# A sigmoid-attention and gated feed-forward kernel: its steps and loads in one table laid out anew

## The chip, the cores and the metric

The kernel runs on one core of a Trainium2 chip. The metric is the device time of one execution in microseconds (us). Before the change it is 368.44 us, the median of three runs (368.12 to 368.74). One further execution was recorded by the hardware profiler; every duration below is from it, and its span, from the first instruction to the last, is 367.6 us.

## The reference, cut to what matters

Sigmoid attention over 8 batches, 12 heads, 448 positions and 64 dimensions; its output, taken as 3584 rows of 768, goes through a two-layer network with a gate:

```python
scores = scale * np.matmul(q, k.transpose(0, 1, 3, 2)) - np.log(S)
attn = 1.0 / (1.0 + np.exp(-scores))
x = np.matmul(attn, v)                        # heads side by side: 3584 x 768
h = x @ w_in                                  # 768 -> 2048
g = h * (1.0 / (1.0 + np.exp(-beta * h)))
out = g @ w_out                               # 2048 -> 768
```

All inputs and the output are fp32. The kernel loads them as fp16 (the DMA casts) and sums in fp32.

## The kernel before, in words

**Units of work.** A batch has 12 heads. Four heads are a quad `g` (three quads a batch, `QPB`), two heads are a slot. The kernel is one long list of steps, in an order written out by hand, that every engine follows for its own part: TensorE (PE), VectorE (DVE), ScalarE (ACT), GpSimd (POOL), and the DMA queues of GpSimd (loads with a cast) and SyncE (SP, the stores). No scheduler moves anything: each engine runs its instructions in the order in which the steps are called, and waits on semaphores for the others. A step is a letter with numbers, and `RUN` (L615) gives the function of each letter:

- `V g.jt` (`visit`, L243): the scores of a quad for one block of 128 keys, 8 or 16 matmuls of 32 rows, into score tiles in PSUM, and on ACT the sigmoid of each (`weigh`, L230). `half_visit` (L259) does the same for half of the queries (224); the first batch uses it.
- `A g` (`attend`, L282): the attention weights times the values, 64 columns wide, for all four key blocks, and the casts to `xT` on DVE (L303). The last block has 64 keys; its matmuls stand at the end, and for odd slots they read a copy of the values' last rows that `double_v_last` (`E`, L148) makes on DVE.
- `D b.dc` and `first_half` (`dense1`, L308): the first layer of batches 0 and 1, six matmuls, a sigmoid on ACT and a product on DVE. `O` (`dense2`, L341) is the second layer of the first two row tiles.
- `I` and `U` (`wino1` L432, `wino2` L530): the two layers of all other rows by seven products for a 2x2 block in place of eight. They need sums of tokens (`X`), of hidden values (`H`) and of weights (`S`, `T`), which DVE makes in fp16 from SBUF (all through `add`, L375), and gates: `G` and `B` (L495, L505) put the product of gate and value on POOL.
- `R g.r` (`transpose`, L194) turns queries (r = 0) or keys (r = 1) on DVE, `Q`, `K` and `load_...` issue loads on POOL's queue.

**PSUM.** `bank` (L89) hands out single banks, the one longest unused first; two score tiles (three in the opening) hold two banks each, so a visit waits until ACT has read the tiles of the visit before. `share_psum` (L76) lays the banks out anew after the opening.

**Tile form of the dense products.** `follow` (L641) looks ahead from each step to the next `V` or `A`. If that is an `A`, `dense` (L171) issues every product as two of 64 columns, the form in which `attend` runs, else as one of 128.

**SBUF rings.** Output tiles `osb` come from a ring of four (`outp`, L63): two for each `I` block or `U` pair, so a tile waits for the store of the one two blocks earlier. Stores go out on SP (L605), 32 rows each except in the last batch. Raw queries and keys have a ring of three, values of two.

**The opening** (L747 to L834) is code, not part of the list: ten matmuls on zeros (`idle_units`), the first quad's casts and turns, all loads up to the first layer's weights, then six half visits with 3, 4, 4, 4, 2 and 2 idle matmuls behind them, the three attends of the first query half with half visits between them, the beta turns, eight loads (L810 to L817: quads 3 and 4, values of batch 1, `w_out` in four parts with quad 5 between), and then the first layer of the first half with the second half's visits and attends between. `follow(STEPS)` runs the rest.

Of the kernel before, what the change touches and what calls it, by code (L numbers as in the profile page):

```python
# [13 lines left out]
def kernel(  # L14
# [267 lines left out]
    def attend(g: int, c0: int, n: int, part=(0, 1)):  # L282
# [4 lines left out]
        avs = [bank("av_ps") for _ in slots]  # L287
        order = sorted(range(JF), key=lambda jt: list(at_tiles).index((slots[-1], jt, c0)))
        todo = [(s, av, jt) for jt in order for s, av in zip(slots, avs)]
        for s, av, jt in todo + [(s, av, JF) for s, av in zip(slots, avs)]:  # L290
            at = at_tiles.pop((s, jt, c0))
            base, nk = (last_base(s), KL) if jt == JF else (0, P)
            for hh in range(2):
                nc.tensor.matmul(  # L294
                    av[hh * D : (hh + 1) * D, 0:n],
                    vs[b][base : base + nk, 2 * (s % NPAIR) + hh, jt],
                    at[base : base + nk, hh, 0:n],
                    start=(jt == order[0]),
                    stop=(jt == JF),
                    tile_position=(base, hh * D),  # L300
                )
        for s, av in zip(slots, avs):
            nc.vector.tensor_copy(out=xTs[b][:, s % NPAIR, c0 : c0 + n], in_=av[:, 0:n])  # L303
# [304 lines left out]
    todo = list(range(NDC))  # L608

    def first_half(n: int):  # L610
        for _ in range(n):
            dense1(0, todo.pop(0), 0, QH)

    ALSO = {g: (g + 1,) if g > QPB and g + 1 < NQUAD else () for g in range(QPB, NQUAD)}
    RUN = {  # L615
        "V": lambda g, jt: visit(g, jt, ALSO[g] if jt == JF else ()),
# [24 lines left out]
    def follow(steps):  # L641
        last_visit = max(i for i, step in enumerate(steps) if step[0] == "V")
        nearer = [""] * len(steps)
        for i in reversed(range(len(steps) - 1)):
            nxt = steps[i + 1][0]
            nearer[i] = nxt if nxt in "VA" else nearer[i + 1]
        for i, (step, then) in enumerate(zip(steps, nearer)):
            tiled["cols"] = D if then == "A" else P
# [5 lines left out]
        R3.1 R3.0 D0.6 D0.12 R4.1 D0.14 D0.7 V3.1 R4.0 D0.13 D0.0 D0.8 V3.0 D0.3 D0.9 V3.3 D0.1  # L654
        D0.10 E1 D0.2 Q6 V3.2 D0.4 O0.0.0 D0.5 O0.0.1 O0.0.2 V4.1 O1.0.0 O0.0.3 A3 V4.0 O1.0.1 R5.1
        D0.11 D0.15 O0.0.4 R5.0 V4.2 O0.0.5 S1.1 O0.0.6 O1.0.2 O1.0.3 S1.0 O0.0.7 S2.0 O1.0.4 V4.3
        O1.0.5 A4 V5.1 O1.0.6 O0.1.0 O0.1.1 O1.1.0 S2.1 Q7 T3.1 O1.0.7 S4.0 T2.1 O0.1.2 V5.0 T3.0
        O0.1.3 O1.1.1 K2 O1.1.2 O1.1.3 O0.1.4 O0.1.5 V5.2 T2.0 O1.1.4 O0.1.6 O0.1.7 R6.1 O1.1.5 R6.0
        A5 O1.1.6 I1.3.1 V6.2 O1.1.7 S4.1 D1.8 R7.0 S3.1 D1.11 T1.1 Q8 V6.0 Q9 D1.3 R7.1 D1.2 X1.0
        V6.1 D1.10 D1.9 E2 K3 D1.1 X1.1 V6.3 T1.0 D1.0 A6 V7.1 I1.3.6 I1.3.2 X1.2 I1.3.5 V7.0 X1.3  # L660
        I1.3.7 I1.3.3 I1.2.1 I1.3.4 G1.3 I1.2.6 B1.3.0 V7.2 R8.1 I1.2.5 I1.2.7 R8.0 B1.3.1 I1.2.2
        I1.2.3 I1.2.4 V8.0 U2.1.0 H2.2 B1.2.1 B1.2.0 R9.1 U2.1.1 R9.0 A7 V8.1 H2.0 H2.1 T4.1 T4.0
        U2.7.0 U2.2.0 U2.2.1 Q10 V8.2 U2.5.0 U2.6.0 U2.6.1 X2.0 S3.0 H2.3 E3 V8.3 U2.5.1 A8 G1.2
        X2.1 V9.1 U2.7.1 U2.3.0 U2.3.1 H4.0 I2.0.1 R10.0 V9.2 H4.2 I2.0.6 U2.4.0 I2.0.5 U2.4.1
        I2.0.2 H4.1 I2.0.3 R10.1 X2.2 U4.1.0 V9.0 X2.3 U4.1.1 Q11 G2.0 U4.6.0 U4.6.1 Q12 A9 V10.0
        I2.0.7 H4.3 U4.5.0 U4.7.0 U4.5.1 V10.1 U4.7.1 I2.0.4 B2.0.1 U4.3.0 U4.4.0 U4.2.0 B2.0.0
        U4.2.1 R11.0 U4.3.1 U4.4.1 R11.1 I2.1.1 V10.2 Q13 Q14 I2.1.6 I2.1.5 I2.1.7 I2.1.2 K4 I2.1.3
        V10.3 I2.1.4 G2.1 B2.1.0 R12.1 I2.2.1 B2.1.1 A10 V11.0 I2.2.6 I2.2.5 R12.0 I2.2.7 I2.2.2
        I2.2.3 I2.3.1 Q15 G2.2 V11.1 I2.3.6 I2.2.4 B2.2.1 B2.2.0 I2.3.5 I2.3.2 R13.1 I2.3.7 I2.3.3
        V11.2 I2.3.4 B2.3.1 U6.1.0 B2.3.0 H6.2 U6.1.1 A11 H6.0 V12.2 U6.2.0 U6.7.0 H6.1 U6.2.1 G2.3  # L670
        V12.0 X3.0 U6.5.0 U6.6.0 U6.6.1 X3.1 U6.5.1 H6.3 I3.0.1 U6.7.1 I3.0.6 X3.2 V12.1 H8.0 E4
        R13.0 U6.3.0 U6.3.1 U6.4.0 U6.4.1 I3.0.5 R15.0 Q16 V12.3 H8.2 I3.0.2 A12 H8.1 V13.1 I3.0.3
        R14.0 U8.1.0 U8.1.1 U8.5.0 U8.6.0 G3.0 I3.0.7 U8.6.1 V13.0 X3.3 R15.1 H8.3 U8.2.0 R14.1
        U8.2.1 U8.5.1 U8.7.0 V13.2 U8.7.1 U8.3.0 I3.0.4 U8.4.0 R16.1 B3.0.0 B3.0.1 U8.3.1 V14.0
        U8.4.1 I3.1.1 A13 V14.1 I3.1.6 K5 I3.1.5 I3.1.7 I3.1.2 I3.1.3 I3.2.1 I3.1.4 Q18 I3.2.6 G3.1
        B3.1.0 B3.1.1 I3.2.2 I3.2.5 V14.2 I3.2.7 I3.2.3 Q17 I3.3.1 I3.2.4 G3.2 I3.3.6 I3.3.5 B3.2.0
        B3.2.1 I3.3.2 I3.3.7 I3.3.3 V14.3 I3.3.4 U10.1.0 B3.3.0 B3.3.1 H10.2 R16.0 U10.1.1 A14 V15.2
        U10.2.0 H10.0 U10.7.0 H10.1 G3.3 U10.2.1 U10.5.0 U10.6.0 U10.6.1 H10.3 U10.5.1 X4.0 V15.0
        U10.7.1 X4.1 U10.3.0 U10.3.1 I4.0.1 I4.0.6 I4.0.5 H12.0 U10.4.0 X4.2 U10.4.1 X4.3 I4.0.2
        I4.0.3 I4.0.7 V15.1 E5 K6 G4.0 Q19 H12.2 U12.1.0 H12.1 U12.1.1 A15 R17.0 V16.1 U12.2.0 R18.1  # L680
        I4.0.4 B4.0.0 U12.6.0 B4.0.1 U12.2.1 U12.5.0 V16.2 U12.6.1 U12.5.1 I4.1.1 H12.3 I4.1.6
        U12.7.0 U12.7.1 R17.1 I4.1.5 U12.3.0 U12.3.1 I4.1.2 V16.0 R18.0 I4.1.3 U12.4.0 I4.1.7
        U12.4.1 Q20 G4.1 V16.3 I4.1.4 A16 B4.1.0 B4.1.1 R19.0 V17.2 I4.2.1 I4.3.1 I4.2.6 I4.2.5
        V17.1 I4.2.2 Q21 I4.2.7 I4.2.3 G4.2 V17.0 I4.2.4 I4.3.6 B4.2.0 I4.3.5 I4.3.7 I4.3.2 B4.2.1
        R20.0 I4.3.3 G4.3 V18.2 I4.3.4 R19.1 A17 I5.0.1 B4.3.0 X5.0 B4.3.1 U14.1.0 V18.0 I5.0.2 X5.1
        I5.0.6 Q22 I5.0.5 U14.1.1 V18.1 X5.2 X5.3 H14.0 I5.0.3 U14.2.0 E6 H14.2 K7 I5.0.7 H14.1
        V18.3 G5.0 U14.2.1 A18 V19.2 I5.0.4 U14.6.0 U14.5.0 U14.7.0 B5.0.0 U14.6.1 U14.5.1 B5.0.1
        U14.7.1 I5.1.1 V19.0 H14.3 I5.1.6 I5.1.2 U14.3.0 R21.1 U14.3.1 R20.1 V19.1 U14.4.0 E7 I5.1.5
        I5.1.7 U14.4.1 I5.1.3 V20.0 R21.0 I5.1.4 G5.1 B5.1.0 I5.2.1 B5.1.1 A19 V20.2 I5.2.6 Q23
        I5.2.5 I5.2.2 I5.2.7 I5.2.3 I5.3.1 I5.2.4 G5.2 I5.3.6 B5.2.0 V20.3 I5.3.5 I5.3.7 B5.2.1  # L690
        I5.3.2 I5.3.3 I5.3.4 V20.1 X6.0 B5.3.1 H16.2 B5.3.0 U16.1.0 U16.1.1 A20 V21.2 U16.2.0 H16.0
        U16.7.0 U16.2.1 G5.3 V21.0 H16.1 U16.5.0 R23.1 U16.6.0 U16.6.1 H16.3 U16.5.1 U16.7.1 H18.2
        I6.0.1 X6.2 V21.1 U16.3.0 X6.1 U16.3.1 U16.4.0 U16.4.1 I6.0.6 R22.1 I6.0.2 R22.0 I6.0.5 A21
        V22.0 H18.0 X6.3 I6.0.3 H18.1 U18.1.0 U18.7.0 U18.1.1 V22.1 I6.0.7 U18.6.0 U18.6.1 V22.2
        I6.0.4 H18.3 U18.5.0 G6.0 U18.2.0 R23.0 U18.5.1 U18.2.1 B6.0.1 B6.0.0 U18.7.1 V22.3 U18.3.0
        U18.3.1 U18.4.0 U18.4.1 I6.1.1 I6.1.6 A22 V23.0 I6.1.5 I6.1.7 I6.1.2 I6.1.3 I6.2.1 G6.1
        I6.1.4 B6.1.0 I6.2.6 I6.2.5 B6.1.1 I6.2.2 V23.1 I6.2.7 I6.2.3 I6.3.1 I6.2.4 I6.3.6 G6.2
        B6.2.1 I6.3.5 B6.2.0 I6.3.7 I6.3.2 I6.3.3 V23.2 I6.3.4 B6.3.1 U20.1.0 H20.2 U20.1.1 A23
        U20.7.0 B6.3.0 U22.1.0 H20.0 U20.2.0 H20.1 X7.0 U20.2.1 U20.5.0 U20.6.0 G6.3 U20.6.1 I7.0.1
        U20.5.1 H20.3 X7.2 U22.1.1 U20.7.1 I7.0.2 X7.1 U20.3.0 U20.3.1 U22.2.0 U22.2.1 H22.0 U20.4.0  # L700
        X7.3 H22.2 H22.1 U20.4.1 U22.5.0 I7.0.6 I7.0.5 U22.7.0 I7.0.7 I7.0.3 U22.6.0 G7.0 I7.0.4
        I7.1.1 I7.1.6 I7.1.5 B7.0.0 B7.0.1 I7.1.2 I7.1.7 I7.2.1 I7.1.3 I7.2.6 G7.1 I7.1.4 I7.2.5
        I7.2.7 B7.1.0 B7.1.1 U22.6.1 I7.2.2 I7.2.3 U22.5.1 H22.3 I7.2.4 I7.3.1 I7.3.6 B7.2.0 I7.3.5
        G7.2 B7.2.1 I7.3.7 U22.7.1 I7.3.2 I7.3.3 U24.1.0 I7.3.4 U22.3.0 U22.3.1 U24.1.1 U22.4.0
        B7.3.0 U22.4.1 U24.2.0 B7.3.1 H24.0 U26.1.0 U24.2.1 H24.1 U24.5.0 G7.3 U24.6.0 H24.2 U24.6.1
        U24.5.1 H24.3 H26.0 U24.7.0 U24.7.1 U26.1.1 U24.3.0 U24.3.1 H26.1 U24.4.0 U26.2.1 U26.5.0
        U26.6.0 H26.2 U26.6.1 U26.5.1 H26.3 U26.7.0 U26.7.1 U24.4.1 U26.3.0 U26.3.1 U26.4.0 U26.4.1
        U26.2.0
# [7 lines left out]
    with tc.manual_schedule():  # L716
# [62 lines left out]
        for g in range(1, QPB):  # L779
            load_one(g, 0, 0, NH)  # L780
            load_one(g, 1)
        load_v(0)
        nc.sync.dma_start(out=beta_in[0:NDC], in_=moe_beta.rearrange("(c p) -> c p", p=P))
        for g in range(QPB - 1):
            load_one(g, 0, NH, NB)
        for c in range(WCH):
            if c == WCH // 2:
                load_one(QPB - 1, 0, NH, NB)
            load_w_in(c)
# [76 lines left out]
```

## Time and profile before

| what | value |
|---|---|
| median of three runs | 368.44 us (368.12 to 368.74) |
| span of the profiled execution | 367.6 us |
| instructions | 9130 |
| HBM read, written | 45.62 MB, 11.01 MB |
| DMA, mean over the span | 95 GB/s |
| PE's last group of matmuls | ends at 364.05 us |
| last store | issued at 364.5 us |

The page gives for each engine its busy time and the share of the span. A group's row gives its line, engine, operation and tiles, how many there are, how long they are busy, the mean of one, and the idle time of the engine before them with what ended it. Matmuls are pipelined, so the times of one overlap with the next; what a matmul costs PE is read from the distance of starts in the timeline. The median of the runs lies 0.84 us above the profiled span; both are needed to turn a sum made in the trace into a time.

### The profile page before, as it was taken

To read this page: it belongs to the slowest core of one execution; us is meant where nothing else is said; L and a number is where in the kernel's file an instruction comes from. 1 tells how busy PE (TensorE), PEld (TensorE's weight loads), DVE (VectorE), ACT (ScalarE), POOL (GpSimd) and SP (SyncE) were. 2 spreads that over 40 slices of the span, in tenths; PEclk is the share of its full clock that TensorE was granted. 3 is DMA by queue.
4 is the path that set the end of the run, shared out by engine and by line. 5 is a ranking of instruction groups with operands and counts; after the bars stand their busy time and mean duration, and the time that the engine had idled before them with its cause. 6 is when DMAs were issued, how large, how long until landed. Compare 5 with 4: busy or idle time off the path is not lost.

```text
span 367.6 us, 9130 instructions
## 1 busy us (share of the span) xinstructions
PE 361.6 (98%) x3677; PEld 237.7 (65%) x3677; DVE 272.2 (74%) x524; ACT 248.7 (68%) x410; POOL 154.3 (42%) x192
## 2 busy tenths in 40 slices
PE   8999999999999999999999999999999999999996
PEld 3478754457465685557757667666856688689763
DVE  4356569889995796876778678868879677778764
ACT  5987976789765797657865579977874859225410
POOL 7834523504413873117761445841630316216610
PEclk9999999999999999999999999999999999999999
DMA  8999999930363890517909363373303030030233
GB/s 163 182 197 201 197 206 199 237 40 2 50 139 52 165 147 2 81 57 122 143 9 153 52 137 51 50 79 88 52 1 88 2 87 2 0 87 0 61 67 134
DMA packets 42698, 34.76 MB, mean 95 GB/s; under 512 B 21904, under 2 KB 39200, under 8 KB 42656
## 3 DMA queue, kind: packets, MB, share of 16 engines
q0 software_dynamic: 36688, 22.47, 44.7%
q1 hardware_dynamic: 5968, 11.71, 11.5%
q8 instruction: 29, 0.48, 0.6%
q14 instruction: 13, 0.11, 0.1%
HBM read 45.62 MB, written 11.01 MB: 154 GB/s over the span
## 4 chain that ended last, share of the span: by engine, by line
PE 94%; DMA 3%; ACT 1%; DVE 1%; SPq 0%; issue 0%; ACTq 0%; DVEq 0%
PE m_ps L174 71%; PE sco L221 12%; PE av_ps L294 10%; DMA out_dram<-osb 2%; PE idle_ps L743 1%; ACT attnT L233 1%; DMA gt<-in_k_dram 1%; DVE osb L375 0%; SPq L605 0%; ACT osb L428 0%; DVE xT L303 0%; ACT osb L466 0%; DVE raw L760 0%; SPq L726 0%; DVE kT L763 0%
## 5 line engine op out<-in xcount | busy, mean ns | idle before, releaser
L233 ACT ACTIVATE attnT<-sco 128x896 f16<-128x896 f32 (+1 forms) x163 | 139.2, 908 | 38.5 <-PE sco L221 37.9
L375 DVE TENSOR_TENSOR osb<-m_ps,osb 128x448 f32<-128x448 f32 (+2 forms) x197 | 116.3, 596 | 51.7 <-PE m_ps L174 42.2
L174 PEld LDWEIGHTS <-w_in 128*128 128x128 f16 (+1 forms) x948 | 81.0, 100 | 19.4 <-issue 11.5
L174 PE MATMUL m_ps<-xT,w_in 128*128 128x224 f16 (+3 forms) x750 | 85.5, 266 | 0.8 <-ACT osb L466 0.5
L495 POOL TENSOR_TENSOR gt<-osb,sg 128x448 f16<-128x448 f32 x26 | 29.5, 1135 | 118.4 <-ACT sg L428 108.2
L505 POOL TENSOR_TENSOR gt<-osb,sg 128x448 f16<-128x448 f32 x52 | 58.3, 1137 | 34.9 <-ACT sg L428 33.2
L428 ACT ACTIVATE sg<-osb,beta_sb 128x224 f32<-128x224 f32 (+1 forms) x104 | 54.0, 575 | 10.0 <-DVE osb L375 9.8
L174 PEld LDWEIGHTS <-sum 128*128 128x128 f16 (+1 forms) x444 | 39.9, 99 | 27.4 <-issue 3.7
L174 PEld LDWEIGHTS <-gt 128*128 128x128 f16 (+1 forms) x474 | 36.9, 102 | 25.8 <-issue 7.7
L174 PE MATMUL m_ps<-w_out,gt 128*128 128x384 f16 (+2 forms) x350 | 52.6, 324 | 0.0
L221 PE MATMUL sco<-qT,kT 32*128 32x448 f16 (+3 forms) x864 | 51.4, 340 | 0.4 <-DVE kT L763 0.2
L174 PEld LDWEIGHTS <-w_S 128*128 128x128 f16 (+1 forms) x486 | 43.9, 99 | 7.0 <-issue 6.0
L174 PE MATMUL m_ps<-w_out,sum 128*128 128x384 f16 (+1 forms) x228 | 40.6, 327 | 0.0
L174 PE MATMUL m_ps<-w_T,sum 128*128 128x384 f16 (+1 forms) x216 | 40.3, 326 | 0.0
L303 DVE CAST xT<-av_ps 128x448 f16<-128x448 f32 (+1 forms) x54 | 28.4, 566 | 14.3 <-PE av_ps L294 14.1
L294 PE MATMUL av_ps<-attnT,v 128*64 128x448 f16 (+3 forms) x400 | 38.2, 343 | 0.0
L174 PE MATMUL m_ps<-xs,w_S 128*128 128x224 f16 (+1 forms) x330 | 36.2, 259 | 0.0
L294 PEld LDWEIGHTS <-v 128*64 128x64 f16 (+1 forms) x432 | 20.5, 108 | 18.1 <-issue 10.2
L428 ACT ACTIVATE osb<-m_ps,beta_sb 128x224 f32<-128x224 f32 x52 | 20.4, 449 | 15.3 <-PE m_ps L174 13.8
L221 PEld LDWEIGHTS <-kT 32*128 32x128 f16 (+1 forms) x864 | 13.4, 96 | 23.1 <-issue 20.9
L466 ACT COPY osb<-m_ps 128x448 f32<-128x448 f32 x26 | 13.8, 536 | 18.4 <-PE m_ps L174 15.4
L135 POOL DMA_DIRECT2D v<-in_v_dram x32 | 19.9, 633 | 13.3 <-DMA w_out<-in_moe_w_out_dram 6.5
(53 smaller groups left out, 300.5 us busy)
## 6 DMA issues: line engine op xcount, KB each, us to landing
out_dram<-osb SPq DMA_DIRECT2D x100, 96.0 KB, 2.6
raw<-in_k_dram POOLq DMA_DIRECT2D x23, 224.0 KB, 5.8
raw<-in_q_dram POOLq DMA_DIRECT2D x21, 224.0 KB, 4.5
v<-in_v_dram POOLq DMA_DIRECT2D x32, 144.0 KB, 7.4
w_in<-in_moe_w_in_dram POOLq DMA_DIRECT2D x8, 384.0 KB, 10.4
w_out<-in_moe_w_out_dram POOLq DMA_DIRECT2D x4, 768.0 KB, 13.1
v<-in_v_dram POOLq DMA_DIRECT2D x16, 48.0 KB, 6.2
out_dram<-osb SPq DMA_DIRECT2D x4, 192.0 KB, 2.6
```

The lines of the kernel that those rows point to most:

```text
L135: queue.dma_start(out=to[i * BLK : (i + 1) * BLK, h0:h1, 0:JF].rearrange("p h j d -> p h (j d)"), in_=rows[:, :, JF * i * D : JF * (i + 1) ...
L174: nc.tensor.matmul(to[c : c + step], hidden[:, c : c + step], weights, **({} if step == P else {"tile_position": (0, c)}), **flags,)
L221: nc.tensor.matmul(sco[base : base + nk, hh, u0 : u0 + n], kT[g][lo : lo + BLK, jt * P : jt * P + nk, e], qT[g][lo : lo + BLK, c0 : c0 + n ...
L233: nc.scalar.activation(out=at[:, :, 0:n], in_=sco[:, :, 0:n], func=AF.Sigmoid, bias=NEG_LOG_S, scale=MSCALE,)
L294: nc.tensor.matmul(av[hh * D : (hh + 1) * D, 0:n], vs[b][base : base + nk, 2 * (s % NPAIR) + hh, jt], at[base : base + nk, hh, 0:n], start ...
L303: nc.vector.tensor_copy(out=xTs[b][:, s % NPAIR, c0 : c0 + n], in_=av[:, 0:n])
L375: nc.vector.tensor_tensor(out=out, in0=in0, in1=in1, op=op)
L428: nc.scalar.activation(out=out, in_=in_, func=AF.Sigmoid, bias=0.0, scale=beta_sb[:, dc : dc + 1])
L466: nc.scalar.copy(out=oa[:, 0], in_=m)
L495: nc.gpsimd.tensor_tensor(out=gt[:, 2 * d : 2 * d + 2, off : off + QH], in0=ob[:, 0], in1=sg, op=ALU.mult)
L505: nc.gpsimd.tensor_tensor(out=gt[:, dc, off : off + S].rearrange("p (h n) -> p h n", h=2), in0=oa[:, :, j], in1=sg, op=ALU.mult,)
L743: nc.tensor.matmul(idle[:, 0:cols], still[:, 0:P], still[:, 0:cols], start=True, stop=True)
```

## The change

**One table.** The opening becomes a list of steps too (`OPENING`), and `follow(OPENING + STEPS)` runs both. `RUN` has new letters: `i` idle matmuls, `h` a half visit, `f` the first layer on the first query half, `r` half a turn, `l`, `k`, `v`, `w`, `o` loads, `b` the beta turns, `p` the PSUM layout. The number of idle matmuls stays at 29; the code ahead of the list stays as it is (the first quad's loads, casts and turns, and the first ten idle matmuls).

**Opening's values in two steps.** `attend` takes a `stage`: `y` does the first three key blocks and keeps the bank (`hold`), `z` the last block, the release and the casts.

```diff
-    def attend(g: int, c0: int, n: int, part=(0, 1)):
+    def attend(g: int, c0: int, n: int, part=(0, 1), stage=(0, 1)):
...
-        avs = [bank("av_ps") for _ in slots]
-        order = sorted(range(JF), key=lambda jt: list(at_tiles).index((slots[-1], jt, c0)))
-        todo = [(s, av, jt) for jt in order for s, av in zip(slots, avs)]
-        for s, av, jt in todo + [(s, av, JF) for s, av in zip(slots, avs)]:
+        if 0 in stage:
+            order = sorted(range(JF), key=lambda jt: list(at_tiles).index((slots[-1], jt, c0)))
+            for s in slots:
+                avs[s, c0] = bank("av_ps", hold=None if 1 in stage else (s, c0)), order[0]
+        todo = []
+        if 0 in stage:
+            todo += [(s, jt) for jt in order for s in slots]
+        if 1 in stage:
+            todo += [(s, JF) for s in slots]
...
+        if 1 not in stage:
+            return
+        for s in slots:
+            av, _ = avs.pop((s, c0))
+            if (s, c0) in held:
+                touch(held.pop((s, c0)))
```

**The look-ahead** sees the new letters, and takes the 64-column form ahead of `y` as well:

```diff
-            nearer[i] = nxt if nxt in "VA" else nearer[i + 1]
+            nearer[i] = nxt if nxt in "VAhyz" else nearer[i + 1]
...
-            tiled["cols"] = D if then == "A" else P
+            tiled["cols"] = D if then in ("A", "y") else P
```

**The order.** The opening's list:

```
i4 l1.0.0 k1 R1.1 l2.0.0 k2 v0 l0.0.1 l1.0.1 w0 w1 i3 i2 w2 w3 r1.0 l2.0.1 w4 w5 w6
h0.0.0 w7 R2.1 h0.0.1 i4 b0 h1.0.0 i4 h1.0.1 r2.0 h2.0.1 r0.1 i2 h2.0.0 y1.0 E0 z1.0
h0.1.1 y2.0 z2.0 r1.1 p0 Q3 Q4 o0.0 K1 o1.0 Q5 o0.1 o1.1 y0.0 z0.0 h0.1.0 f1 f0 f2
h1.1.0 f4 f5 f3 f6 h1.1.1 r2.1 f7 y0.1 z0.1 h2.1.0 f8 f9 f10 f11 h2.1.1 y1.1 z1.1
f12 y2.1 z2.1 f13
```

Nine of the 19 later idle matmuls (`i4`, `i3`, `i2`) now stand ahead of the first half visit `h0.0.0`. The rest of the table holds the same steps as before in another order; of the places that the prediction speaks of, these rows are before and after:

```
before  ... U8.3.0 I3.0.4 U8.4.0 ... U8.4.1 I3.1.1 A13 V14.1 I3.1.6 K5 ... Q18 ... Q17 I3.3.1 ...
after   ... I3.0.5 K5 A12 ... V13.2 Q18 ... U8.3.1 U8.4.0 B3.0.0 U8.4.1 A13 V14.1 I3.1.6 ...
before  ... V5.2 T2.0 O1.1.4 O0.1.6 O0.1.7 R6.1 O1.1.5 R6.0 A5 O1.1.6 I1.3.1 V6.2 ...
after   ... T3.0 T2.0 O1.1.1 O0.1.5 O1.1.2 R6.0 X1.0 O0.1.6 O1.1.3 V5.2 R6.1 T3.1 S2.1 O0.1.7
        O1.1.4 O1.1.5 T1.0 O1.1.6 A5 Q8 R9.1 V6.2 O1.1.7 K3 T1.1 D1.11 T2.1 S3.1 R7.1 ...
before  U26.7.0 U26.7.1 U24.4.1 U26.3.0 U26.3.1 U26.4.0 U26.4.1 U26.2.0
after   U26.7.0 U26.7.1 U26.3.0 U24.4.1 U26.4.0 U26.3.1 U26.4.1 U26.2.0
```

The fp16 sums (`X`, `H`, `S`, `T`) are placed at other steps than `G` and `B`, whose products run on POOL. What each step computes is the same.

## The prediction

> **What bounds the kernel now.** I read the page's first part, then the chain, then PE's waits.
>
> ```profile
> span 367.6 us, 9130 instructions
> ...
> PE 361.6 (98%) x3677; PEld 237.7 (65%) x3677; DVE 272.2 (74%) x524; ACT 248.7 (68%) x410; POOL 154.3 (42%) x192
> ...
> PE 94%; DMA 3%; ACT 1%; DVE 1%; SPq 0%; issue 0%; ACTq 0%; DVEq 0%
> ```
>
> PE is busy for 361.6 of 367.6 us and is 94% of the chain. What is left is 1.19 us ahead of the first matmul, some waits, and the last store. So the change can win only what PE loses inside its work, and can lose anywhere. PE's waits:
>
> ```profile
> PE idle_ps L743 <- DVE gt L736: 1.2, 1, 1.2
> PE m_ps L174 <- ACT osb L466: 0.5, 1, 0.5
> PE m_ps L174 <- ACT attnT L233: 0.2, 1, 0.2
> PE sco L221 <- DVE kT L763: 0.2, 1, 0.2
> PE sco L221 <- ACT attnT L233: 0.2, 1, 0.2
> ```
>
> After 19.4 us only the 0.5 us counts. The timeline between 177 and 182 us shows what is behind it:
>
> ```profile
> 177.51 0.79 ACT L428 ACTIVATE osb<-m_ps,beta_sb 128x224 f32<-128x224 f32 x2 [1.23 <-DMA out_dram<-osb]
> ...
> 178.53 1.31 PE L174 MATMUL m_ps<-xs,w_S 128*128 128x224 f16 x12
> ...
> 179.78 0.55 ACT L466 COPY osb<-m_ps 128x448 f32<-128x448 f32 x1
> ...
> 180.38 1.31 PE L174 MATMUL m_ps<-xT,w_in 128*128 128x224 f16 x12 [0.54 <-ACT osb L466]
> ...
> 181.77 0.73 PE L174 MATMUL m_ps<-xT,w_S 128*128 128x224 f16 x6
> ```
>
> ACT waits 1.23 us for a store to leave its output tile, so the copy at 179.78 is late and PE waits for it. Twelve such matmuls take 12 x 0.096 = 1.15 us; from 178.53 to 180.38 they took 1.85, from 180.38 to 181.77 1.39: 0.70 + 0.24 = 0.94 us lost. The stores are late because the loads of K5 (in the order, just behind U8's last stores) share the DMA engines: between 165 and 180 us stores take 2.9 to 6.0 us to land, against 1.8 where nothing loads.
>
> **Part 1, opening: +0.8 us.** PE's and ACT's timelines before:
>
> ```profile
> 1.19 4.03 PE L743 MATMUL idle_ps<-gt 128*128 128x512 f16 x10 [1.19 <-DVE gt L736]
> 5.42 0.58 PE L221 MATMUL sco<-qT,kT 32*128 32x224 f16 x16 [0.20 <-DVE kT L763]
> ...
> 19.37 2.46 PE L174 MATMUL m_ps<-xT,w_in 128*128 128x224 f16 x24 [0.21 <-ACT attnT L233]
> ```
> ```profile
> 6.04 6.28 ACT L233 ACTIVATE early<-sco 128x896 f16<-128x896 f32 x8 [0.87 <-PE sco L221]
> 12.46 3.06 ACT L233 ACTIVATE attnT<-sco 128x896 f16<-128x896 f32 x4
> 16.15 3.17 ACT L233 ACTIVATE attnT<-sco 128x896 f16<-128x896 f32 x4 [0.62 <-PE sco L221]
> ```
>
> From 6.04 to 15.5 us ACT never stops: it reads score tiles, and PE's half visits wait for it. The first product of the first layer (19.37) follows ACT's 16th sigmoid. After the change nine warm idle matmuls (0.216 us each from start to start, 1.04 for four with the change of form) come ahead of the first half visit: it starts at 4.95 + 0.11 + 9 x 0.216 + 0.10 = 7.10 instead of 5.42, and ACT's first sigmoid at 7.71 instead of 6.04, 1.67 late. I walk on with the distances of before. Sigmoids 1 to 8 keep their rhythm (the idle matmuls between them are the same 4 and 4): the eighth ends at 14.0. h2.0.1 needs the tile of the seventh (13.56): its sigmoids run from 14.36, those of h2.0.0 from 15.86 to 17.58. y1.0 and z1.0 stand on PE meanwhile (15.9 to 16.8; v landed at 14.05, its copy is done by 15.0). h0.1.1 starts at 16.85, its first sigmoid ends at 18.52. By the order's semaphores y0.0 waits for that one, for the new PSUM layout reuses the bank: 18.57. y0.0, z0.0 and h0.1.0 take 1.4 us, and f1 also waits for z0.0's two casts (0.7 us behind its last matmul): the first layer starts in effect at **20.2 instead of 19.37**. Behind it both kernels have the same first-layer work, and I find no step in which PE waits more than 0.1 us. Bounds: if ACT never waited for PE (14 sigmoids and their pitches of 0.81 and 0.43 from 7.71), y0.0 could start at 17.2, that is -0.5; if every hand-over costs another 0.1, +1.3.
>
> **Part 2, PE's own work: -0.4 us.** A matmul in the form of the one before costs 96 ns at 224 columns; going from one form to another costs about 0.1 us: from 22.27 to 24.10 us there are 18 matmuls and one change, 18 x 0.096 + 0.10 = 1.83.
>
> ```profile
> 22.27 1.90 PE L174 MATMUL m_ps<-xT,w_in 128*128 128x224 f16 x18
> 24.10 0.74 PE L221 MATMUL sco<-qT,kT 32*128 32x224 f16 x16
> ```
>
> Counting forms in the two orders from the first layer on: 189 changes before, 186 after, -0.3 us. The look-ahead also splits 104 more products in two of 64 columns; a pair takes 162 to 163 ns at 384 columns and 95 to 96 at 224, one whole 163 and 96: -0.1 at most, I take it. Bounds 0 to -0.5.
>
> **Part 3, the waits of the steady part: -1.05 us.** K5 now stands ahead of A12 and Q18 behind V13.2, some 13 and 7 us of PE's work ahead of U8's last stores; those then land in about 1.9 us and the 0.94 us go. Another 0.11 goes at 44.36, where PE's first `w_out` matmul waits for its load: o0.0 is now issued ahead of K1, which by the landings of before puts it at 40.4. For what is late next I compared every wait of PE with PE's work between it and its source. The shortest such distances are alike in both orders (1.25 us from a product to the use of its bank, 1.4 from an attend to its `xT`). The stores' tightest new place is U10.3.1 to U12.1.1, 5.5 us against 6.7 before, where the store landed 1.6 us early; 0.4 is left. I take no new wait there, with +0.5 as its bound.
>
> The fp16 sums away from POOL's products: 0. DVE waits little for POOL:
>
> ```profile
> DVE osb L375 <- PE m_ps L174: 42.2, 58, 2.2
> ...
> DVE sum L375 <- POOL gt L505: 1.2, 2, 0.7
> ```
>
> and it idles 42.2 us waiting for PE, so what a sum saves is covered. The Trainium skill, "SBUF — State Buffer", section "Who interferes with whom", says that a VectorE instruction with two SBUF inputs contends with a GpSimd instruction that reads SBUF, and that whichever issues first holds the pair while the other fully blocks. The trace agrees in that one sum alone overlaps a product by over 0.1 us (799 ns against 685); by the rule a meeting would cost up to a product's 1.14 us, and eight of them 9 us of VectorE, still less than its 42.2 us.
>
> **Part 4, a crowded queue of sums: +0.1.** Between 60 and 66 us the new order gives DVE, without a gap, T2.0, R6.0, X1.0, R6.1, T3.1, S2.1, an `osb` copy and T1.0, and then A5's two casts, which D1.11 needs 0.04 us after I expect them. I take 0.1; see the second rival.
>
> **Part 5, tail: +0.5 us.** The stores' last 864 KB flow without a gap at about 370 GB/s from 363.4 to 365.9. U24.4.1, whose 384 KB store opens that run, now comes one U part (four matmuls, 0.65 us) later, while PE's end stays. That delays the last landing by 0.5; bounds 0 and 0.65.
>
> **Sum.** +0.8 - 0.4 - 1.05 + 0.1 + 0.5 = -0.05: a span of 367.55, and with the 0.84 us between span and median **368.4 us**. From the bounds: -2.6 to +3.0 if all fell together.
>
> **Rivals.**
> - *The opening keeps ACT's pace* (faster). Then part 1 is -0.5 in place of +0.8: 367.1. For it: ACT, not PE, sets the opening's pace, and the new order puts visits next to each other. Against it: the walk above used the hand-overs that the trace shows.
> - *DVE's queue becomes the bound at 60 to 77 us* (slower). DVE is busy for 7.2 of the 8 us from 60 to 68 before, with four weight sums of 0.95 us there; now there are five, and three in place of two in the 8 us behind. By distances of starts the eight pieces of part 4 take 5.4 us, by their durations 6.3; the truth is between, and from 0.04 us on PE pays. At full durations PE loses 0.8 at D1.11 and 0.5 more before 77 us, +1.3: 369.7. Against it: starts are what a queue shows when it is full.
> - *The sums and products are not set apart in effect*, or were already: then no term changes, 368.4 too.
>
> **How the numbers follow.** A measurement can tell 0.2% (0.74 us) from no change. Forecast with its near cases, 367.7 to 369.2: 0.37. First rival, alone or with a smaller tail, 366.5 to 367.7: 0.33. Second rival or a store that comes late, over 369.2: 0.30. Those are the chances of same, faster, slower. The range leaves out 0.1 on either side: 366.8 to 370.0; the forecast's own is 367.7 to 369.2.
>
> **What would show it.** Part 1: the first `w_in` matmul at 20.2, ACT's first sigmoid at 7.7. Part 2: 0.1 us at each change. Part 3: no ACT wait for `out_dram<-osb` near 177, no PE wait for the copy behind it. Part 4: PE's wait on `xT` near 66. Part 5: 4.05 us from PE's end to the span's end, against 367.6 - 364.05 = 3.55. Wrong if PE shows a wait over 0.5 us that none of these names.

## The result, and the profile after

The changed kernel takes 372.64 us, the median of six executions (370.63 to 376.37). Against before the ratio is 1.0092, 95% interval 1.0065 to 1.012: slower by some 3.4 us, where 368.4 was predicted. The ratio leaves out disturbed executions (376.37 among them), so it is lower than that of the two medians. The profiled execution took 371.86 us at a span of 370.0. The lines of its page that answer to those shown of before:

```profile
span 370.0 us, 9330 instructions
...
PE 362.4 (98%) x3781; PEld 239.9 (65%) x3781; DVE 276.1 (75%) x524; ACT 247.9 (67%) x410; POOL 155.1 (42%) x192
...
PE 91%; POOL 2%; DVE 2%; DMA 1%; ACT 1%; issue 1%; SPq 0%; DVEq 0%; POOLq 0%
```

PE's share of the chain falls from 94 to 91%; POOL and DVE now have 2% each. PE's waits (in total, times, longest):

```profile
PE sco L221 <- ACT early L233: 1.5, 2, 0.9
...
PE m_ps L174 <- DVE sum L389: 0.6, 1, 0.6
PE m_ps L174 <- DVE xT L317: 0.6, 1, 0.6
PE sco L221 <- ACT attnT L233: 0.3, 1, 0.3
```

None of the first three stood before, the last was 0.2, and the 0.5 us for the copy at 180 us is gone. Put together by starts of matmuls in the two traces:

| us | before | after | difference |
|---|---|---|---|
| start to the first `w_in` matmul | 19.37 | 21.58 | +2.21 |
| from there to the start of the last matmul | 344.42 | 344.90 | +0.48 |
| from there to the end of the span | 3.78 | 3.56 | -0.22 |

The last row goes by the traces' spans to the hundredth, 367.57 and 370.04; with the rounded spans it is 3.81 and 3.52, and so the expectations below have it.

**The opening.** PE's timeline after:

```profile
7.46 0.67 PE L221 MATMUL sco<-qT,kT 32*128 32x224 f16 x18
9.04 0.69 PE L221 MATMUL sco<-qT,kT 32*128 32x224 f16 x14 [0.91 <-ACT early L233]
...
13.97 0.69 PE L221 MATMUL sco<-qT,kT 32*128 32x224 f16 x14 [0.64 <-ACT early L233]
...
16.43 1.66 PE L303 MATMUL av_ps<-early,v 128*64 128x224 f16 x16
...
21.58 2.09 PE L174 MATMUL m_ps<-xT,w_in 128*128 128x224 f16 x18
```

The first half visit starts at 7.46, not 7.10, and at 16.43 sixteen matmuls of the values take 1.66 us where such a group took 1.02 before. The trace's record of the granted clock says why: full clock from 5.62 us (4.89 before), half clock again from 15.858 to 19.271 us, 3.413 us, then full until PE is done. Before has no such stretch while PE works; its clock falls only at 366.70 us, behind the last matmul. The windows view, cut at multiples of 3.413 us from 5.62 (PE's busy time comes first, the granted clock behind the five engines):

```profile
9.03:12.45 3.42, 3.41 (x46) 1.42 (x45) 1.80 (x7) 3.27 (x5) 2.65 (x5) 1.00 1.69 183
12.45:15.85 3.40, 2.38 (x44) 0.96 (x40) 0.77 (x2) 3.04 (x5) 3.31 (x5) 1.00 1.40 193
15.86:19.27 3.41, 3.41 (x50) 1.81 (x44) 0.69 (x2) 2.05 (x4) 2.07 (x4) 0.50 1.40 173
```

In the stretch that holds the waits ahead of h2.0.1 and h2.0.0 PE was busy for 2.38 us; the next one ran at 0.50.

**The wait at 204.98 us.** The chain of waits between 198 and 206 us:

```profile
198.41 5.31 DMA out_dram<-osb
...
204.31 0.62 DVE xT L317
204.98 1.14 PE m_ps L174 x6
```

A store of U10, 5.3 us on its way, keeps its output tile; DVE's copy for U12.1.1 waits for it, and A15's casts wait behind the copy. On POOL's queue Q19's first load is issued just ahead of those stores, whose row on SyncE's queue follows, and before it was not:

```profile
196.09 0.58 POOL L115 DMA_DIRECT2D raw<-in_q_dram  x1
```
```profile
196.89 6.33 SPq L619 DMA_DIRECT2D out_dram<-osb  x8
```
```profile
202.10 1.14 POOL L495 TENSOR_TENSOR gt<-osb,sg 128x448 f16<-128x448 f32 x1 [7.74 <-DVE sum L375]
203.18 0.62 POOL L115 DMA_DIRECT2D raw<-in_q_dram  x1
```

The last two rows are before: Q19 stood behind the product of G4.0, which held POOL's queue for 7.74 us.

**The wait at 351.58 us.** DVE's and POOL's rows after:

```profile
349.20 1.60 DVE L389 TENSOR_TENSOR sum<-gt 128x1024 f16<-128x1024 f16 x1 [0.23 <-POOL gt L519]
```
```profile
349.12 1.14 POOL L509 TENSOR_TENSOR gt<-osb,sg 128x448 f16<-128x448 f32 x1
```

The sum H24.0 starts when POOL ends B7.3.1's product, and so does the next product, G7.3. The sum takes 1.60 us; its kind takes 0.69. Two steps later PE has waited 0.77 us (start to start, against its usual distance).

My theory: three causes, the nine early idle matmuls (over 2 us), Q19's new place (0.7 or more) and G7.3's new place (0.77), while the gain at 180 us belonged mostly to the one execution that I had profiled.

### The profile page after: what moved, and what is told of

Read it like the earlier page. It is cut to its first block, busy times and chain, and to the rows that moved or that the text cites. A ratio compares the mean times of both kernels' runs of the same rounds, so it can differ in the third digit from the quotient of the medians.

```text
span 370.0 us, 9330 instructions
## 1 busy us (share of the span) xinstructions
PE 362.4 (98%) x3781; PEld 239.9 (65%) x3781; DVE 276.1 (75%) x524; ACT 247.9 (67%) x410; POOL 155.1 (42%) x192
## 4 chain that ended last, share of the span: by engine, by line
PE 91%; POOL 2%; DVE 2%; DMA 1%; ACT 1%; issue 1%; SPq 0%; DVEq 0%; POOLq 0%
PE m_ps L174 68%; PE sco L221 12%; PE av_ps L303 10%; PE idle_ps L789 2%; POOL gt L519 2%; DMA out_dram<-osb 1%; ACT early L233 1%; DVE sum L389 1%; DVE osb L389 1%; SPq L619 0%; ACT attnT L233 0%; ACT sg L442 0%; DVE xT L317 0%; DVE gt L782 0%; DVE osb L584 0%
## 5 line engine op out<-in xcount | busy, mean ns | idle before, releaser
L174 PE MATMUL m_ps<-xT,w_in 128*128 128x224 f16 (+2 forms) x792 | 85.0, 265 | 0.0
L442 ACT ACTIVATE sg<-osb,beta_sb 128x224 f32<-128x224 f32 (+1 forms) x104 | 54.8, 578 | 5.8 <-DVE osb L389 5.7
L303 PEld LDWEIGHTS <-v 128*64 128x64 f16 (+1 forms) x432 | 21.4, 110 | 17.7 <-issue 9.6
L337 DVE TENSOR_TENSOR gt<-m_ps,sg 128x224 f16<-128x224 f32 (+1 forms) x40 | 16.1, 430 | 11.3 <-ACT sg L334 11.2
```

The costliest lines, as they stand in the source:

```text
L174: nc.tensor.matmul(to[c : c + step], hidden[:, c : c + step], weights, **({} if step == P else {"tile_position": (0, c)}), **flags,)
L303: nc.tensor.matmul(av[hh * D : (hh + 1) * D, 0:n], vs[b][base : base + nk, 2 * (s % NPAIR) + hh, jt], at[base : base + nk, hh, 0:n], start ...
L337: nc.vector.tensor_tensor(out=gt[:, dc, off : off + n], in0=m1[:, 0:n], in1=sg[:, 0:n], op=ALU.mult)
L442: nc.scalar.activation(out=out, in_=in_, func=AF.Sigmoid, bias=0.0, scale=beta_sb[:, dc : dc + 1])
```

## The opening: four kernels

**e1: the old opening ahead of the new list.**

```diff
-        i4 l1.0.0 k1 R1.1 l2.0.0 k2 v0 l0.0.1 l1.0.1 w0 w1 i3 i2 w2 w3 r1.0 l2.0.1 w4 w5 w6
-        h0.0.0 w7 R2.1 h0.0.1 i4 b0 h1.0.0 i4 h1.0.1 r2.0 h2.0.1 r0.1 i2 h2.0.0 y1.0 E0 z1.0
...
+        h0.0.0 i3 h0.0.1 i4 h1.0.0 i4 h1.0.1 i4 h2.0.0 i2 h2.0.1 i2 E0 r0.1 y0.0 z0.0
+        h0.1.0 y1.0 z1.0 h0.1.1 r1.1 y2.0 z2.0 b0 Q3 Q4 K1 o0.0 o1.0 Q5 o0.1 o1.1 p0
...
```

> The changed kernel with the opening of before written as a table (idle matmuls behind the half visits, quads and values in the old order; two first-layer products left to the later list, which stays the changed one). The trace of the changed kernel has its first w_in matmul at 21.58 us against 19.37, and from there to PE's last matmul 344.90 us against 344.42, and 3.52 against 3.81 us behind that. Theory A (the opening alone is the loss, the rest of the list is even): first w_in matmul at 19.3 to 19.6, no stretch at half clock behind 5 us, span 367.8, median 368.6, that is +0.2 over before, with the waits near 203 and 349 us (0.74 and 0.77) still there. Rival (the later list loses, too, and the opening only hides it): above 369.3. Second rival (the late opening makes the waits near 205 and 351 as well): these go with it, median 367.2.

Measured: 373.95 us, ratio 1.0136 (1.0111 to 1.0161), span 370.3: no faster than the changed kernel (372.64; the intervals overlap). In the profiled execution the first `w_in` matmul came at 19.73 and the clock stayed full (three of the other five have a mean clock of 0.995, that of one half-clock stretch), but PE had a new wait at 44.08 us:

```profile
PE m_ps L174 <- DMA w_out<-in_moe_w_out_dram: 1.9, 1, 1.9
```

None of the three theories named this. The new list begins its second layer 22.3 us behind the first `w_in` matmul (43.91 - 21.58 after the change) where before had 25.0 (44.36 - 19.37), and needs the first part of `w_out` issued ahead of K1, as the new opening has it. So e1 says nothing of what the opening costs, only that its load order and the list belong together; the waits at 205 and 352 us were there (0.80 and 0.78).

**e2: only the nine idle matmuls put back.**

```diff
-        i4 l1.0.0 k1 R1.1 l2.0.0 k2 v0 l0.0.1 l1.0.1 w0 w1 i3 i2 w2 w3 r1.0 l2.0.1 w4 w5 w6
-        h0.0.0 w7 R2.1 h0.0.1 i4 b0 h1.0.0 i4 h1.0.1 r2.0 h2.0.1 r0.1 i2 h2.0.0 y1.0 E0 z1.0
+        l1.0.0 k1 R1.1 l2.0.0 k2 v0 l0.0.1 l1.0.1 w0 w1 w2 w3 r1.0 l2.0.1 w4 w5 w6
+        h0.0.0 i3 w7 R2.1 h0.0.1 i4 b0 h1.0.0 i4 h1.0.1 i4 r2.0 h2.0.1 r0.1 i2 h2.0.0 i2 y1.0 E0 z1.0
```

> The changed kernel, and in its opening only the nine idle matmuls put back behind the half visits (3, 4, 4, 4, 2, 2). Theory A (the nine idle matmuls ahead of the first half visit are the cause, first by making ACT's sigmoids 1.7 us late and then by the half clock that PE's gaps bring): first half visit at 5.4, ACT's first sigmoid at 6.0, full clock from 5 us on, first w_in matmul at 19.4 to 20.0, median 368.6 to 369.2. Rival (the new order of visits, values and turns in the opening is the cause): the first w_in matmul stays over 21 and the median over 370.2.

Measured: 369.68 us, ratio 1.0030 (1.0020 to 1.0041); first half visit at 5.62, first `w_in` matmul at 19.38, no half clock in 11 executions. The median is 0.5 above the forecast, but 0.62% (2.3 us) of the 0.92% are gone with nothing but the idle matmuls moved. The rival falls. PE's rows of the first half visit and of the first `w_in` matmul in e2:

```profile
5.62 0.94 PE L221 MATMUL sco<-qT,kT 32*128 32x224 f16 x16 [0.19 <-DVE kT L809]
...
19.38 2.09 PE L174 MATMUL m_ps<-xT,w_in 128*128 128x224 f16 x18
```

**e3: gaps filled, the nine still early.**

```diff
-        h0.0.0 w7 R2.1 h0.0.1 i4 b0 h1.0.0 i4 h1.0.1 r2.0 h2.0.1 r0.1 i2 h2.0.0 y1.0 E0 z1.0
+        h0.0.0 i4 w7 R2.1 h0.0.1 i4 b0 h1.0.0 i4 h1.0.1 i4 r2.0 h2.0.1 r0.1 i4 h2.0.0 y1.0 E0 z1.0
```

> The changed kernel with ten more idle matmuls in the gaps in which PE waits for ACT in the opening (four between the two halves of quad 0's first visit, four ahead of h2.0.1, two more ahead of h2.0.0); the nine early ones stay. Theory A's two parts come apart: if the half clock is what costs, it goes and 1.2 of the 2.2 us come back, first w_in matmul at 20.4, median 370.6; the later start of ACT's chain stays. Rival (the clock does not matter, since ACT sets the pace there): the first w_in matmul stays at 21.4 to 21.6 and the median at 371.8. Second rival (all is the clock): 19.5, 369.6.

Measured: first half visit at 7.41, first `w_in` matmul at 20.32 (20.4 expected), full clock in all six executions; 371.4 us, ratio 1.0067 (1.0052 to 1.0082). The opening came out as the theory has it, 1.26 us earlier than after the change. The time fell by 0.25% only, and the intervals overlap. In the two profiled executions the store's wait took half of it back: PE lost 1.39 us at 204.34 here and 0.74 after the change. Whether that holds for the other executions is not shown.

**e4: the kernel before, its nine idle matmuls early.**

```diff
+        idle_units(4)
+        idle_units(3)
+        idle_units(2)
         for n in range(2 * QPB):
             half_visit(n // 2, 0, n % 2)
-            idle_units((3, 4, 4, 4, 2, 2)[n])
+            if n in (1, 2, 4):
+                idle_units((0, 4, 4, 0, 2, 0)[n])
```

> The kernel before, and in it only nine of the nineteen later idle matmuls moved ahead of the first half visit (0, 4, 4, 0, 2, 0 stay behind the visits). Theory A: ACT's first sigmoid at 7.7 in place of 6.0, PE waits over 0.5 us ahead of two visits, a stretch of 3.4 us at half clock in most executions, first w_in matmul at 20.8 to 21.5, median 369.8 to 370.6. Rival (order of visits and values is the cause, idle matmuls only fill): within 0.3 us of before, 368.4.

Measured: 370.25 us, ratio 1.0037 (1.0020 to 1.0054), first `w_in` matmul at 20.57, PE's waits of 0.91 and 0.63 us in the same two places. Half clock in 2 of 12 executions (not in the profiled one), fewer than I expected. The early idle matmuls alone cost the old kernel 1.4 us.

**e12: the gap ahead of h2.0.1 alone filled.** This asks what brings the half clock.

```diff
-        h0.0.0 w7 R2.1 h0.0.1 i4 b0 h1.0.0 i4 h1.0.1 r2.0 h2.0.1 r0.1 i2 h2.0.0 y1.0 E0 z1.0
+        h0.0.0 w7 R2.1 h0.0.1 i4 b0 h1.0.0 i4 h1.0.1 i4 r2.0 h2.0.1 r0.1 i2 h2.0.0 y1.0 E0 z1.0
```

> The changed kernel with four more idle matmuls at one place only, ahead of h2.0.1; the 0.91 us wait of PE ahead of h0.0.1's third score tile stays. In both traces of the changed kernel the half clock begins three stretches of 3.413 us after the clock has risen, and the stretch just before it holds the waits ahead of h2.0.1 and h2.0.0 (0.64 and 0.28 us) and only two idle matmuls; the one with the 0.91 us wait was followed by full clock. Theory A (what counts is how much PE does in the stretch before): no execution with a mean clock of 0.995, where the changed kernel has them in 5 of 7; profiled first w_in matmul at 20.3 to 20.6, median 371.0 to 371.6, as e3. Rival (the 0.91 us wait counts as well): half clock in a third of the executions or more.

Measured: no half clock in six executions; the 0.91 us wait was there and did nothing. The windows, cut as before, from the clock's rise at 7.19:

```profile
14.02:17.42 3.40, 3.12 (x48) 1.44 (x47) 0.77 (x2) 2.89 (x5) 3.08 (x5) 1.00 1.36 174
17.43:20.83 3.40, 3.35 (x72) 2.16 (x70) 1.83 (x6) 2.62 (x4) 1.08 (x2) 1.00 1.41 185
```

With 3.12 us of work in place of 2.38 the next stretch stays at full clock: filling this one gap is enough. But theory A is too simple. Later in the same trace a stretch with 1.58 us of work, less than 2.38, is followed by full clock as well:

```profile
205.16:208.57 3.41, 1.58 (x10) 0.97 (x10) 2.70 (x5) 1.34 (x2) 0.00 (x0) 1.00 0.02 6
208.58:211.98 3.40, 3.40 (x30) 1.95 (x28) 0.35 (x1) 2.65 (x7) 3.13 (x3) 1.00 0.00 0
```

The time missed the forecast: 372.55 us, ratio 1.0093 (1.0069 to 1.0117). In the profiled execution the clock rose late, the first half visit came at 8.23 and the first `w_in` matmul at 21.14; and store waits took 0.96 us at 114.51 and 2.27 at 206.99. So it is shown which gap lets the half clock in, but not what of PE's work counts. What it costs in time is less sure: the changed kernel's two executions at full clock took 370.63 and 370.65 us and its others 371.86 or more, but e12, always at full clock, took 371.73 to 373.88. The 1.2 us for it below is read from traces of the opening.

## The two waits behind the opening: three kernels

All three start from e2, whose opening has no half clock.

**e5: Q19 behind G4.0.**

```diff
-        U10.4.1 I4.0.7 U12.1.1 Q19 A15 V16.1 I4.0.4 B4.0.0 B4.0.1 U12.5.0 U12.2.0 R18.0
-        U12.6.0 G4.0 U12.2.1 I4.1.1 ...
+        U10.4.1 I4.0.7 U12.1.1 A15 V16.1 I4.0.4 B4.0.0 B4.0.1 U12.5.0 U12.2.0 R18.0
+        U12.6.0 G4.0 Q19 U12.2.1 I4.1.1 ...
```

> The kernel of e2 (the changed one with the nine idle matmuls put back, 1.003 times before) and one step moved: Q19, the loads of quad 19, from ahead of A15 to behind G4.0. In the changed kernel's trace Q19's two loads are issued at 196.1 and 196.7 us, just ahead of the stores of U10 (from 196.9), of which one takes 5.3 us to land; VectorE's copy into that output tile waits for it, the casts of A15 behind the copy are late, and PE waits 0.66 to 1.39 us near 203 to 205. Before, Q19 stands behind G4.0, whose product holds GpSimd's queue until 202, and is issued at 203.2. Theory A (Q19 in front of the stores is the cause): that wait goes, 0.7 us or more, median 369.0 or less. Rival (K6, the values' loads at 192.4 to 195.5, does it, and it stands nearly where it stood before): the wait stays over 0.5 and the median at 369.7.

Measured: 369.07 us, ratio 1.0006 (0.9996 to 1.0017), 0.24% below e2. PE goes on at 203.03, the place of the wait, without one; K6 stands where it stood. Theory A holds, but for the median, forecast at 369.0 or less. (The profiled execution had a wait of 1.21 us at 112.82, for a store that took 7.7 us.) PE's rows around the place:

```profile
202.44 0.75 PE L174 MATMUL m_ps<-xs,w_in 128*128 128x224 f16 x6
203.03 0.81 PE L174 MATMUL m_ps<-w_out,sum 128*128 128x384 f16 x4
```

**e6: G7.3 behind U24.2.1.**

```diff
-        U22.3.1 U24.2.0 H24.0 U22.4.0 H24.1 U22.4.1 G7.3 U24.2.1 U24.6.0 U24.5.0 U24.6.1
+        U22.3.1 U24.2.0 H24.0 U22.4.0 H24.1 U22.4.1 U24.2.1 G7.3 U24.6.0 U24.5.0 U24.6.1
```

> The kernel of e2 and one step moved: G7.3 from ahead of U24.2.1 to behind it, so that ScalarE makes its sigmoid, and GpSimd its product, only after ScalarE's copy for U24.2.1. In the changed kernel the sum H24.0 (released when GpSimd ends the product of B7.3.1) and the product of G7.3 (next in GpSimd's queue) start together, at 349.20 and 349.12, and the sum takes 1.60 us where its kind takes 0.69; PE waits 0.77 us for the sums behind it, in every trace. Theory A (VectorE's sum is blocked by GpSimd's product): the sum takes 0.69 us, the wait goes, median 368.9. Rival (the sum is late by its release, the product before it, and not by the meeting): the sum takes 1.6 us again or PE still waits over 0.5 us there, median 369.7.

Measured: 369.33 us, ratio 1.0007 (0.9987 to 1.0028), 0.23% below e2; the two intervals overlap, so the times alone would not settle it. In the trace H24.0 takes 0.69 us and PE has no wait behind it. Its release is the same product as before (0.23 us of waiting in both), so the meeting was the cause of the long sum and of PE's wait, not the release.

**e8: e2, e5 and e6 together**, the diffs of the three.

> The changed kernel with the idle matmuls put back (e2), Q19 behind G4.0 and G7.3 behind U24.2.1 together. If the three causes add up: 1.4 us below e2, with no wait of PE over 0.3 us behind 19.4 us, median 368.2, that is 0.5 below before (PE's own work is 0.4 us less). Rival (each mended place uncovers another wait near it): at or above before, 368.7 to 369.3.

Measured: 368.01 us, ratio **0.9981 (0.9972 to 0.9991)**, faster than before. 0.49% below e2, near the sum of the two (0.24 + 0.23). Page, PE's waits and DVE's row of the sum in e8:

```profile
span 366.5 us, 9330 instructions
```
```profile
PE sco L221 <- DVE qT L199: 0.4, 1, 0.4
...
PE sco L221 <- ACT attnT L233: 0.3, 1, 0.3
```
```profile
346.48 0.69 DVE L389 TENSOR_TENSOR sum<-gt 128x1024 f16<-128x1024 f16 x1 [0.23 <-POOL gt L519]
```

The waits that are left lie in the opening.

**e11: e8 with K4 later.**

```diff
-        V9.1 X2.1 U2.7.1 U2.3.0 U2.3.1 Q11 I2.0.1 K4 U2.4.0 H4.0 X2.2 V9.2 R10.0 I2.0.6 H4.2
-        U2.4.1 I2.0.5 U4.1.0 R10.1 V9.0 H4.1 I2.0.2 I2.0.3 U4.1.1 U4.6.0 Q12 U4.6.1 A9 X2.3
+        V9.1 X2.1 U2.7.1 U2.3.0 U2.3.1 Q11 I2.0.1 U2.4.0 H4.0 X2.2 V9.2 R10.0 I2.0.6 H4.2
+        U2.4.1 I2.0.5 U4.1.0 R10.1 V9.0 H4.1 I2.0.2 I2.0.3 U4.1.1 U4.6.0 Q12 U4.6.1 K4 A9 X2.3
```

> The kernel of e8 (0.998 times before) and K4, the values' loads of batch 4, moved from behind I2.0.1 to behind U4.6.1. In the kernels of e5 and e6 VectorE's copy near 111 us waited for a store that took 7.7 us to land, and PE lost 0.9 to 1.2 us at 112; K4's six loads are issued at 101.7 to 105.4, among those stores (102.4 to 108.6). If these loads make the stores late: no wait at 112, the upper executions go, median 367.7 to 367.9. Rival (the other loads there, of quads 11 and 12, are enough): 368.0, as e8.

Measured: 368.06 us, ratio 0.9979 (0.9967 to 0.9991): as e8. The profiled execution has no wait at 112, but one execution cannot show that a wait that comes and goes is gone; the times leave it open.

## What the wait at 180 us was worth: two kernels

**e7: before, with only K5 and Q18 moved.**

```diff
-        R13.0 U6.3.0 U6.3.1 U6.4.0 U6.4.1 I3.0.5 R15.0 Q16 V12.3 H8.2 I3.0.2 A12 H8.1 V13.1 I3.0.3
+        R13.0 U6.3.0 U6.3.1 U6.4.0 U6.4.1 I3.0.5 R15.0 Q16 V12.3 H8.2 I3.0.2 K5 A12 H8.1 V13.1 I3.0.3
...
-        U8.2.1 U8.5.1 U8.7.0 V13.2 U8.7.1 U8.3.0 I3.0.4 U8.4.0 R16.1 B3.0.0 B3.0.1 U8.3.1 V14.0
-        U8.4.1 I3.1.1 A13 V14.1 I3.1.6 K5 I3.1.5 I3.1.7 I3.1.2 I3.1.3 I3.2.1 I3.1.4 Q18 I3.2.6 G3.1
+        U8.2.1 U8.5.1 U8.7.0 V13.2 Q18 U8.7.1 U8.3.0 I3.0.4 U8.4.0 R16.1 B3.0.0 B3.0.1 U8.3.1 V14.0
+        U8.4.1 I3.1.1 A13 V14.1 I3.1.6 I3.1.5 I3.1.7 I3.1.2 I3.1.3 I3.2.1 I3.1.4 I3.2.6 G3.1
```

> The kernel before and only K5 moved ahead of A12 and Q18 behind V13.2, as in the changed kernel. Theory A (the 0.94 us that PE lost at 178 to 182 us belong to the one profiled execution, whose span of 367.6 lies 0.9 above the usual 366.7 of before): the median stays within 0.3 of before, and what falls are the executions of before over 369. Rival (the prediction's term: the wait stands in all executions): 0.9 below before, 367.8.

Measured: 368.39 us, ratio 0.9994 (0.9984 to 1.0004): 0.2 us, by the interval between none and 0.6, not 0.94. In its trace (span 366.3) PE loses nothing between 178 and 182 us; the groups of twelve start 1.15 us apart, which is 12 x 0.096:

```profile
178.45 1.31 PE L174 MATMUL m_ps<-xs,w_S 128*128 128x224 f16 x12
179.60 1.31 PE L174 MATMUL m_ps<-xT,w_in 128*128 128x224 f16 x12
180.75 0.74 PE L174 MATMUL m_ps<-xT,w_S 128*128 128x224 f16 x6
```

**e9: before, once more, unchanged.**

> The kernel before, unchanged, profiled once more. Theory A (the profiled execution that the prediction was made from was a long one): span 366.4 to 367.0, PE's last matmul at 362.8 to 363.2 against 363.79, no wait of PE over 0.4 us between 178 and 182 us, and 3.5 us from the last matmul's start to the span's end in place of 3.81. Rival (the wait at 180 us belongs to the kernel): it is there again, 0.5 us or more, and the span is 367.4 or more.

Measured: 369.39 us at a span of 367.4. The chain near 180 us, and ACT's row:

```profile
171.73 5.70 DMA out_dram<-osb
...
181.87 0.73 PE m_ps L174 x6
```
```profile
177.60 0.79 ACT L428 ACTIVATE osb<-m_ps,beta_sb 128x224 f32<-128x224 f32 x2 [0.93 <-DMA out_dram<-osb]
```

ACT's wait for the store is there again, 0.93 us in place of 1.23, but PE loses 0.24 us at 181.87 and none at 180, in place of 0.94. So theory A is right on PE's loss and wrong on the span: this execution was long, too, by other things (the clock rose at 7.03 us, the first `w_in` matmul came at 19.75, and PE lost 0.47 us at 45.11 to the load of `w_out`). Over 33 executions of before beside e5 to e8 the spans run from 366.2 to 368.1, one of 370.4 aside, with a median of 366.9.

**e10: the changed kernel, once more, unchanged.**

> The changed kernel, unchanged, profiled once more. By the theory the first half visit starts at 7.4, the first w_in matmul at 20.3 to 20.6 if no stretch at half clock falls into the opening and at 21.5 if one does; the wait near 203 to 205 us is there with 0.6 to 1.4 us, and the sum at 349 us takes 1.6 us and costs PE 0.77, exactly as in the other traces. Rival: these two waits belong to single executions like the one at 180 us before; then one of them is missing.

Measured: 372.92 us at a span of 371.1. Half clock again, from 16.84 us on; first half visit at 7.95, first `w_in` matmul at 22.05; waits of 1.33 us at 206.03 and 0.78 at 352.65. All three causes are there again, so they belong to the kernel and not to one execution; the expected 21.5 was low since the clock rose later, at 6.60.

## Why the prediction failed, point by point

**The ground of the sum failed: "a span of 367.55, and with the 0.84 us between span and median 368.4 us".** I took the distance from the profiled span to the median of other executions as a constant of the kernel. Where both are known for one execution, its time lies 1.8 to 2.0 us above its span (369.39 and 367.4, 371.86 and 370.0, 372.92 and 371.1). So the execution that I had profiled took about 369.6 us by estimate (367.6 and 2.0), 1.1 above the median, and I subtracted its mishaps as gains. (The bounds beside it do not add up either: those of the five parts, with the second rival's 1.3 in part 4, give -2.05 to +2.7, not -2.6 to +3.0. By the ratio the change cost 3.4.)

**Part 1 (+0.8) failed in its first term: "nine warm idle matmuls (0.216 us each ...)", first half visit at 7.10.** Its trace had the clock up at 4.89, and I took that as given. In the traces here it rises between 4.59 and 7.19 us. Ahead of that an idle matmul takes 0.427 us, and all nineteen now stand ahead of the first half visit. It starts at 7.20 with the rise at 4.88 (e4), 7.46 with 5.62, 7.95 with 6.60, 8.23 with 7.19; the old order starts it at 5.42 and 5.43 with 4.89 and 7.03. The walk behind it was right: 13.1 us from there to the first layer's start; in e3 and e12, whose filled gaps keep the clock full, the first `w_in` matmul comes 12.91 and 12.90 us behind the half visit, and 0.20 more goes just behind it. But with the half clock, which I did not consider at all, it is 14.12 (after) and 14.11 (e10): another 1.2 us. So in the changed kernel's trace 0.36 us of the miss lie in the start and 1.2 in the half clock, and the opening cost 2.2 and 2.7 us (after, e10) against the old profile. Its upper bound, +1.3, was made of hand-overs alone. Of the rivals, the one that I gave 0.33 (the opening keeps ACT's pace) had the wrong sign.

**Part 2 (-0.4): the sign and the counts right, the size half.** The traces have the 189 and 186 changes of form and the 104 more split products. From the first `w_in` matmul to the last matmul e7 (the old list) takes 343.32 us and e11 (the new one) 343.49. But by the distances of starts e11 loses 0.37 us to five small waits among its 128-column products (0.20 at 19.58 and 0.08 at 66.47 the longest), e7 none. Without them the new list is 0.20 shorter in these two executions; no run isolates it.

**Part 3 (-1.05) failed three times.** The 0.94 us were mis-sized: the mechanism is right (the wait goes with K5 moved) but the median gains 0.2, which the interval does not tell from none (e7); the 0.11 us at 44.36 went as forecast. The store's "tightest new place", U10.3.1 to U12.1.1, was named with +0.5 as its bound and taken as none: PE lost 0.74 (after), 1.33 (e10), 0.66 (e2), 1.39 (e3), 0.80 (e1), 2.27 (e12) and 3.54 us (e6) there, in all seven traces of the new list with Q19 early. I had compared PE's distances and the old landing times, and not asked where Q19 stands in POOL's queue: ahead of G4.0's product, it is issued 7 us earlier, into those stores. And "the fp16 sums away from POOL's products: 0" rested on the idle time that DVE has in all. One sum with PE waiting for it has no idle time to spend. Sums that ran over 0.1 us long beside a product: one before (799 ns), six after (831, 1011, 1194, 1369, 1477 and 1601 ns), of which only the last, at 349.20, cost PE anything, 0.77 us. The change sets sums and products apart in its list of steps, but not on the clock. The rule of the Trainium skill that I weighed, "SBUF — State Buffer", "Who interferes with whom", holds here: the product that issued first ran its 1.14 us undisturbed, to 350.26, and the sum, which had started 0.08 us behind the product, ended 0.54 us behind its end, most of its own 0.69.

**Part 4 (+0.1): right.** PE loses 0.08 us at D1.11, at 68.77; that rival did not happen.

**Part 5 (+0.5) failed.** From the last matmul's start to the span's end the new list takes 3.56 us and the old one 3.53 (e7, e9) and 3.54 (e4): no cost. The old profile's 3.78 was one execution's. There SyncE took 1.65 us over the issue at 361.40, in e7 0.81 over the same one; but in e4 it took 1.38 and the end was no later, so what made that end late stays open.

**The sum as it came.** From the usual span of before, 366.9, to the 370.0 of the one trace: opening about +2, the store's wait +0.7, the sum's +0.8, K5 -0.2 make 3.3, against 3.1. By the ratios: 0.92% for the change, of which 0.62 go with the idle matmuls, 0.24 with Q19 and 0.23 with G7.3; that would be 0.17 below before, and e8 is 0.19 below.

## What to carry to other kernels

Before you subtract a wait that one trace shows, ask whether the median has it: compare that execution's own time with the others, and treat waits for a DMA landing as a spread, not a number. When a load is moved, look at what it stood behind on its own queue; a slow instruction there may have been what kept it away from the stores. Matmuls that only keep the clock up must stand where PE would wait: put ahead of the work, they are paid for, and the gaps that they leave can cost the clock.

## What the runs showed of the hardware

- **The clock goes by stretches of 3.413 us.** It rose between 3.4 and 6.0 us behind the first matmul (1.19 us), and every half-clock stretch while PE had work (after, e10, e6) lasted 3.413 us. The Trainium skill, "TensorE: Matmul & The Clock Gate", "Part 1: The HAM clock gate", has a free-running window of 3413 ns, and the traces agree.
- **PE's busy time alone does not tell whether the clock stays.** In the stretch just before half clock it was 2.38 us (after), 2.37 (e10) and 0.67 (e6, whose profiled execution has a wait of 3.4 us at 205.83). Stretches with 2.49 (e12), 2.50 (e10), 2.51 (after) and 2.56 (e4) were followed by full clock, but so were some with less: 1.58 (e12, from 205.16 us), 1.95 (e1, from 40.23) and 2.24 (e10, from 204.58). Those three hold dense products almost alone. In the two of the opening score matmuls, of 32 rows, take 1.90 (after) and 1.82 us (e10). That score matmuls count for less would fit; no run tests it. The Trainium skill, on the same page, section "HAM oscillation — how this bites in real kernels", gives as the abstract rule no idle gap over about 3.4 us; in the two stretches of the opening the longest single wait was 0.64 us, so by the measurements shorter waits can suffice.
- **A store's landing varies widely beside loads.** The stores in these chains took 5.3 (after), 5.7 (e9), 7.0 (e12), 7.2 (e4), 7.7 (e5) and 8.3 us (e6), at 198, 172, 199, 153, 104 and 196 us, where the medians of those traces are 1.9 to 2.5. They hit different places in different executions, which would make a kernel with several tight places spread: the spans of e8 lie within 0.8 us (365.8 to 366.6), those of the changed kernel between 368.8 and 372.1, one of 374.6 aside. Part of that spread is the half clock.
